# The first batch of a fused attention and MoE kernel: q norms as column sums on the tensor engine, and A^T W in column parts of 128, 256 and 384

## The chip, the cores and the metric

One core of one Trainium2 chip. The metric is the device time of one execution in microseconds (us), the median of several; lower is better. A profile is of one execution, and its span starts a little inside the metric (572.1 us of span for a run of 573.92). Engines in the profile: PE is the tensor engine (matmuls), PEld its weight loads, DVE the vector engine, ACT the scalar engine, POOL GpSimd, SP the sync engine. POOL issues nearly all of the input loads here. The matmuls of this kernel write to PSUM tiles (`..._ps`), in PSUM banks, and ACT and DVE copy the results out ("evacuate" them). `wo` is the weight of the output product. All runs used below are in the fast state.

## The reference

```python
# B, N, C = 4, 6144, 256; d_ff = 768; 24576 tokens
qn = q / (norm(q, axis=1, keepdims=True) + 1e-06)      # each column of q[b] (6144 rows) by its norm
kn = k / (norm(k, axis=1, keepdims=True) + 1e-06)
s = kn.transpose(0, 2, 1) @ qn / tau                    # 256 x 256 a batch
a = exp(s - s.max(-1)); a /= a.sum(-1) + 1e-09
x = (v @ a).reshape(B * N, C)
h = maximum(maximum(x @ w1, x @ w2), x @ w3)
out = h @ w_out
```

## The kernel before

The kernel never forms x. It multiplies the 256 x 256 attention matrix into the three weights once a batch (A^T W, `aw`), then computes h = max over m of v times `aw[m]` by blocks of 128 hidden columns (`fc` = 0 to 5) for each chunk of 512 tokens, then the output product with `wo`. In the first batch nothing can hide the way to `aw`: q has to land, the gram matrix k^T q has to be summed, the softmax done, the first part of A^T W multiplied, and only then can the first h matmul run. That stretch is what the change is about.

```python
    for load, widths in ((load_k, [8] * 5), (load_q, [8] * 4 + [4, 4, 4, 2, 2])):
        ...                                   # q of batch 0 lands in nine pieces
    FT = 2 * P                                # P = 128
    def load_w(fp):
        fsl = slice(fp * FT, (fp + 1) * FT)
        for wt, w in zip(w_sb, w_list):
            POOL.dma_start(out=wt[:, :, fsl], in_=w.rearrange("(cc p) f -> p cc f", p=P)[:, :, fsl])
    load_v(0)
    for fp in range(d_ff // FT):
        load_w(fp)
    load_v(1)
    wo_sb = consts.tile([P, FC, d_model], BF16, name="wo_sb")
    ...
    def gram(b):                              # for batch 0 only
        ...
        for tp in range(NG // 2):             # 24 pairs of row groups
            for j in range(CC):               # CC = 2 halves of the 256 columns
                PE.matmul(ps[j][:, 0:C], lhsT=qt[:, tsl, jsl], rhs=kt[:, tsl, :], ...)
                PE.matmul(ps[j][:, C:C + P], lhsT=qt[:, tsl, jsl], rhs=qt[:, tsl, jsl], ...)   # q by q
    ...
    def softmax_t(ps, rkb):
        for j in range(CC):                   # the norms: the diagonal of q by q
            DVE.tensor_tensor_reduce(out=scr, in0=ps[j][:, C:C + P], in1=ident, scale=1.0, scalar=0.0,
                                     op0=ALU.mult, op1=ALU.add, accum_out=n2q[:, j:j + 1])
        ACT.activation(out=lnq, in_=n2q, func=AF.Ln)
        ACT.activation(out=rq, in_=lnq, func=AF.Exp, scale=-0.5, bias=neg_ln_tau)
        return exp_t(scaled([ps[j][:, 0:C] for j in range(CC)], rkb), rq)     # et, one Exp per half j
    ...
    def aw_first(et, aw):                     # part of 256 columns, six products in six PSUM banks
        products(0, (0, 1))                   # j = 0, m = 0 and 1
        sums(0)
        sums(1)                               # row sums of et
        DVE.reciprocal(out=rinv, in_=rs_ps[:, 0:CC])
        products(1, (0, 1))
        for j in range(CC):
            products(j, (2,))
        ...                                   # evacuate the six, scaled by rinv, on ACT and DVE in turn
    ...
    ps = gram(0)
    ...                                       # six dummy matmuls
    et = softmax_t(*ps)
    v_transpose_pe(0)
    aw = alloc_aw()
    rinv = aw_first(et, aw)
    v_transpose(1)                            # a DMA transpose of the second v chunk
    hold_loads(1)                             # POOL waits for that transpose
    POOL.dma_start(out=wo_sb, in_=moe_w_out.rearrange("(fc p) d -> p fc d", p=P))
    load_v(2)
    load_v(3)
    ...                                       # then the chunks; the other parts of A^T W follow h blocks 0 and 2
```

## Time and profile before

| | before |
|---|---|
| time, median of 4 fast runs beside the changed kernel | 574.11 us (574.0 to 574.3) |
| last q piece lands | 33.63 us |
| first h matmul | 37.52 us, 3.89 after it |
| wo lands | 50.54 us |
| first output product | 50.63 us, 17.00 after the last q piece |

From the page of the kernel before: the busy line of the engines, and PE's row of the view in 40 slices (each digit the busy share of 14.3 us in tenths).
```profile
PE 553.9 (97%) x3349; PEld 330.7 (58%) x3350; DVE 411.1 (72%) x647; ACT 309.1 (54%) x539; POOL 235.1 (41%) x240
PE   3799999999999999999999999999999999999997
```
PE is full from the third slice to the last but one, so whatever is gained must be gained in the first two to three slices, and it reaches the end only if it moves the start of the unbroken row of matmuls.

The first h matmul in PE's timeline of the kernel before (the chain has it at 37.56, as it shows modelled ends):
```profile
37.52 1.46 PE L389 MATMUL h_ps<-vt_sb,aw_sb 128*128 128x512 bf16 x6
```

### The profile page before, as it was taken

Reading aid. Unit: us, or ns where it says so; the run is one execution under the profiler, and the core shown is the slowest. Engines: PE = TensorE matmul, PEld = TensorE weight load, DVE = VectorE, ACT = ScalarE, POOL = GpSimd, SP = SyncE. Lnnn points to the kernel's source line nnn. Section 1 sums busy time; section 2 is a strip of 40 time slices with the busy share of each in tenths; the row PEclk is TensorE's granted clock in tenths of the full one; section 3 lists DMA queues with packets and bytes.
Section 4 is the critical chain, followed back from the end, with each engine's and each line's share of the span. In section 5 each row is a group of like instructions: output and inputs, shape, how many; then the busy total and the mean of one; then the engine's idle time right before and its main releaser. Section 6 shows DMA issues by size and latency. Waiting matters only on the chain.

```text
span 572.1 us, 9442 instructions
## 1 busy us (share of the span) xinstructions
PE 553.9 (97%) x3349; PEld 330.7 (58%) x3350; DVE 411.1 (72%) x647; ACT 309.1 (54%) x539; POOL 235.1 (41%) x240
## 2 busy tenths in 40 slices
PE   3799999999999999999999999999999999999997
PEld 2665555555755555555575555555575555555566
DVE  0048777877577777777768777777868778778775
ACT  1044567677454576776545467767645444444443
POOL 2443357776730078776560048777750000000000
PEclk9999999999999999999999999999999999999999
DMA  9998998884598168984179339885437323132112
GB/s 143 106 146 129 136 237 126 159 135 116 99 107 160 56 107 158 134 148 110 57 128 151 99 81 140 148 141 98 124 86 154 75 75 109 56 103 64 56 55 76
DMA packets 76960, 65.64 MB, mean 115 GB/s; under 512 B 52464, under 2 KB 62576, under 8 KB 76784
## 3 DMA queue, kind: packets, MB, share of 16 engines
q0 software_dynamic: 19072, 26.48, 38.7%
q1 hardware_dynamic: 57696, 38.41, 23.7%
q8 instruction: 26, 0.43, 0.3%
q14 instruction: 22, 0.18, 0.1%
q10 hardware_dynamic: 144, 0.13, 0.1%
HBM read 78.64 MB, written 25.17 MB: 181 GB/s over the span
## 4 chain that ended last, share of the span: by engine, by line
PE 93%; DMA 5%; POOL 0%; issue 0%; DVE 0%; POOLq 0%
PE h_ps L389 65%; PE o_ps L409 22%; DMA q_sb<-in_q_dram 5%; PE gram L260 3%; PE ew_ps L311 3%; POOL k_sb L99 0%; PE o_ps L434 0%; PE ew_ps L335 0%; PE warm_ps L469 0%; PE vt_ps L372 0%; PE gram L177 0%; PE n_ps L215 0%; DVE ht_sb L395 0%; DVE o_sb L461 0%; PE n_ps L217 0%
## 5 line engine op out<-in xcount | busy, mean ns | idle before, releaser
L389 PE MATMUL h_ps<-vt_sb,aw_sb 128*128 128x512 bf16 (+1 forms) x1764 | 406.7, 375 | 0.1
L389 PEld LDWEIGHTS <-aw_sb 128*128 128x128 bf16 x1764 | 171.8, 98 | 161.3 <-DVE aw_sb L317 2.0
L394 DVE TENSOR_TENSOR s_mx<-h_ps,s_mx 128x512 bf16<-128x512 f32 (+1 forms) x294 | 198.7, 676 | 87.1 <-ACT s_mx L393 86.8
L393 ACT ACTIVATE s_mx<-h_ps 128x512 bf16<-128x512 f32 (+1 forms) x294 | 172.4, 587 | 124.9 <-PE h_ps L389 124.0
L395 DVE TENSOR_TENSOR ht_sb<-h_ps,s_mx 128x512 bf16<-128x512 f32 (+1 forms) x294 | 200.2, 681 | 31.4 <-PE o_ps L409 0.5
L203 POOL TENSOR_TENSOR acc<-acc,sq 128x768 f32<-128x768 f32 x90 | 147.6, 1651 | 70.5 <-ACT sq L197 61.6
L409 PE MATMUL o_ps<-wo_sb,ht_sb 128*128 128x256 bf16 x1128 | 153.9, 273 | 0.0
L409 PEld LDWEIGHTS <-ht_sb 128*128 128x128 bf16 x1128 | 110.4, 98 | 52.0
L412 ACT ACTIVATE o_sb<-o_ps 128x512 f32<-128x512 f32 x94 | 56.1, 597 | 85.3 <-PE o_ps L409 85.3
L110 POOL DMA_DIRECT2D v_sb<-in_v_dram x48 | 27.5, 578 | 37.7 <-DMA vt_sb<-v_sb 35.5
L197 ACT ACTIVATE sq<-q_sb 128x768 bf16<-128x768 fp8e4 x48 | 40.5, 845 | 0.0
L197 ACT ACTIVATE sq<-k_sb 128x768 bf16<-128x768 fp8e4 x48 | 40.1, 835 | 0.0
L200 POOL CAST acc<-sq 128x768 f32<-128x768 bf16 x6 | 4.9, 823 | 68.7 <-ACT sq L197 68.7
L102 POOL DMA_DIRECT2D q_sb<-in_q_dram x33 | 18.4, 564 | 5.1 <-DMA v_sb<-in_v_dram 4.1
L165 PE MATMUL kk<-k_sb 128*128 128x256 fp8e4 x48 | 7.5, 338 | 11.9 <-DVE k_sb L151 6.3
L99 POOL DMA_DIRECT2D k_sb<-in_k_dram x29 | 16.1, 555 | 3.1 <-DMA v_sb<-in_v_dram 1.2
L260 PE MATMUL gram<-k_sb,q_sb 128*128 128x512 fp8e4 x144 | 16.8, 277 | 0.0
L260 PEld LDWEIGHTS <-q_sb 128*128 128x256 fp8e4 x144 | 15.9, 136 | 0.6
L314 ACT ACTIVATE aw_sb<-ew_ps,rinv 128x384 bf16<-128x384 f32 (+1 forms) x24 | 13.2, 555 | 5.5 <-PE ew_ps L311 4.7
L311 PE MATMUL ew_ps<-w_sb,et 128*128 128x384 bf16 (+1 forms) x96 | 15.6, 313 | 0.0
L177 PE MATMUL gram<-k_sb,q_sb 128*128 128x512 fp8e4 x48 | 11.4, 332 | 2.6 <-DMA q_sb<-in_q_dram 2.4
L165 PEld LDWEIGHTS <-k_sb 128*128 128x256 fp8e4 x48 | 6.4, 182 | 12.9 <-DMA k_sb<-in_k_dram 6.6
(67 smaller groups left out, 112.9 us busy)
## 6 DMA issues: line engine op xcount, KB each, us to landing
out_dram<-o_sb SPq DMA_DIRECT2D x41, 512.0 KB, 2.9
v_sb<-in_v_dram POOLq DMA_DIRECT2D x48, 256.0 KB, 4.2
k_sb<-in_k_dram POOLq DMA_DIRECT2D x24, 192.0 KB, 6.0
q_sb<-in_q_dram POOLq DMA_DIRECT2D x24, 192.0 KB, 7.6
out_dram<-o_sb SPq DMA_DIRECT2D x13, 256.0 KB, 2.0
k_sb<-in_k_dram POOLq DMA_DIRECT2D x5, 256.0 KB, 10.8
w_sb<-in_moe_w_dram POOLq DMA_DIRECT2D x9, 128.0 KB, 5.7
kf<-in_k_dram SPq DMA_DIRECT2D x1, 1024.0 KB, 4.8
```

Source lines behind the costliest of these rows:

```text
L102: POOL.dma_start(out=qk[b][0][:, g0:g0 + w, :], in_=q_r[b][:, g0:g0 + w, :])
L110: POOL.dma_start(out=t, in_=v_r[gi // NCH, gi % NCH])
L197: ACT.activation(out=sq, in_=src, func=AF.Square)
L203: POOL.tensor_tensor(out=acc, in0=acc, in1=sq, op=ALU.add)
L260: PE.matmul(g[:, j * C:(j + 1) * C], lhsT=qt[:, tsl, j * P:(j + 1) * P], rhs=kt[:, tsl, :], start=(tp == 0 and j == 0), stop=(tp == NG // ...
L311: PE.matmul(ew[:, :w], lhsT=et[:, j, ic * P:(ic + 1) * P], rhs=w_sb[m][:, j, fsl], start=(j == 0), stop=(j == CC - 1))
L389: PE.matmul(t.rearrange("p (t n) -> p t n", n=P), lhsT=aw[m][:, ic, fsl], rhs=vt[:, tsl, ic, :], start=(ic == 0), stop=(ic == CC - 1))
L393: ACT.activation(out=s_mx, in_=hp[0], func=AF.Copy)
L394: DVE.tensor_tensor(out=s_mx, in0=hp[1], in1=s_mx, op=ALU.max)
L395: DVE.tensor_tensor(out=ht, in0=hp[2], in1=s_mx, op=ALU.max)
L409: PE.matmul(st["ps"][:, half], lhsT=ht[:, fc, t * P:(t + 1) * P], rhs=wo_sb[:, fc, :], start=(fc == 0), stop=(fc == FC - 1))
L412: ACT.activation(out=st["o"][:, t - 1:t + 1, :].rearrange("p t d -> p (t d)"), in_=st["ps"], func=AF.Copy)
```

## The change

Its intent: the q norms should come sooner than the DVE diagonal gives them, and the first h matmul should need only 128 columns of A^T W, since the first h block uses no more. Squares of each q piece are made on ACT and DVE, and PE sums their columns with one-column matmuls, while it waits for the next piece. The 256-column part that follows is put between the matmuls of the first h block, and the last 384 columns behind h block 2. The PE transposes of the first v chunk use two PSUM banks, so that DVE and ACT copy out at the same time.

```diff
-    FT = 2 * P
+    PARTS = ((0, P), (P, 3 * P), (3 * P, d_ff))
+    def load_w(lo, hi): ...                      # three loads a part, of 128, 256 and 384 columns
...
-                PE.matmul(ps[j][:, C:C + P], lhsT=qt[:, tsl, jsl], rhs=qt[:, tsl, jsl],
-                          start=False, stop=last, perf_mode=DR, skip_group_check=True)
+        def squares(g0, w):
+            ACT.activation(out=a[:, 0:h, :], in_=ra, func=AF.Square)
+            DVE.tensor_tensor(out=d[:, 0:h, :], in0=rd, in1=rd, op=ALU.mult)
+        def columns(rows, first=False, last=False):
+            for n, (t, r) in enumerate(rows):
+                for j in range(CC):
+                    PE.matmul(nq[:, j:j + 1], lhsT=t[:, r, j * P:(j + 1) * P], rhs=ones_c, ...)
+        for i, w in enumerate(QW):               # columns of the piece before, gram of this one, squares
...
-    def softmax_t(ps, rkb):
-        for j in range(CC):
-            DVE.tensor_tensor_reduce(...)
+    def softmax_first(gs, rkb, n2q):             # n2q is the bank of column sums
...
     def aw_first(et, aw):
-        products(0, (0, 1))
-        sums(0)
-        sums(1)
+        for j in range(CC):
+            for ic in range(CC):
+                PE.matmul(rs_ps[:, ic:ic + 1], lhsT=et[:, j, ic * P:(ic + 1) * P], rhs=ones_c, ...)
+            for m, ic, ew in ews:
+                product(et, ew, m, ic, *PARTS[0], js=(j,))
         DVE.reciprocal(out=rinv, in_=rs_ps[:, 0:CC])
-        products(1, (0, 1))
-        for j in range(CC):
-            products(j, (2,))
...
     def v_transpose_pe(gi):
-        vt_ps = xtile("vt_ps", cols=TPC * C, dtype=BF16)
+        banks = [xtile("vt_ps", cols=TPC * C, dtype=BF16), ps_h.tile([P, TPC * C], BF16, tag="h", name="vt_ps2")]
...
+    def h_block_first(aw, et, rinv):
+        for m in range(3):
+            ...                                  # two h matmuls of m
+            for ic in range(CC):
+                product(et, ews[m][ic], m, ic, *PARTS[1])
+        ...                                      # evacuations between the three steps of the maximum
...
-    for i in range(6):                           # dummy matmuls
+    for i in range(2):
...
-                        gaps[2 * fp - 2].append(lambda fp=fp: aw_part(et, rinv, aw, fp, FT))
+                    gaps[2].append(lambda: aw_part(et, rinv, aw, *PARTS[2]))
```

## The prediction

> **What bounds the kernel now.** I read the page first, then the chain of waits, then the timeline of the first 52 us, then the list of DMA landings. PE is busy 553.9 us of 572.1, and the only waits of PE that the waits view lists are on k and q loads and on the first cast. So from the first h matmul on PE is never short of work, and only the first 38 us can give something back. The chain of waits, in order of time (start us, us, what):
> ```profile
> 20.91 12.72 DMA q_sb<-in_q_dram
> 33.63 0.04 issue
> 33.67 0.32 PE gram L177
> ...
> 34.29 1.24 PE warm_ps L469 x5
> 35.53 0.45 PE vt_ps L372 x8
> 35.98 0.61 PE ew_ps L335 x4
> 36.59 0.08 PE rs_ps L329 x4
> 36.67 0.89 PE ew_ps L335 x8
> 37.56 1.41 PE h_ps L389 x6
> 38.97 1.31 PE ew_ps L311 x12
> 40.28 2.66 PE h_ps L389 x12
> 42.94 1.31 PE ew_ps L311 x12
> 44.25 6.54 PE h_ps L389 x30
> 50.80 0.66 PE o_ps L409 x6
> ```
> The last q piece lands at 33.63. From there to 37.5 the softmax runs, and dummy matmuls stand in for work. Then PE is solid: h, A^T W, h, and at 50.6 the first output product. The timeline of the softmax (start us, us, engine, line, operation):
> ```profile
> 34.09 0.29 DVE L282 CUSTOM_DVE_ANT_0 scr<-gram,ident 128x128 f32<-128x128 f32 x1 [14.01 <-PE gram L179]
> 34.75 0.75 DVE L268 TENSOR_TENSOR e_in<-gram,rkb 128x256 f32<-128x256 f32 x2
> 34.87 0.20 ACT L286 ACTIVATE lnq<-n2q 128x2 f32<-128x2 f32 x1 [6.00 <-DVE n2q L282]
> 35.34 0.91 ACT L275 ACTIVATE et<-e_in,rq 128x256 bf16<-128x256 f32 x2
> 36.70 0.17 DVE L341 RECIPROCAL rinv<-rs_ps 128x2 f32<-128x2 f32 x1 [0.27 <-PE rs_ps L329]
> ```
> The norm's diagonal (34.09 to 34.83 on DVE) holds up both Ln and e_in, so it costs about 0.7 us on the path. The third thing to see is the first output product, which needs wo:
> ```profile
> 45.36 0.83 POOL L483 DMA_DIRECT2D wo_sb<-in_moe_w_out_dram  x1
> ...
> 50.42 0.75 PEld L409 LDWEIGHTS <-ht_sb 128*128 128x128 bf16 x6
> 50.63 0.82 PE L409 MATMUL o_ps<-wo_sb,ht_sb 128*128 128x256 bf16 x6
> ```
> ```profile
> wo_sb<-in_moe_w_out_dram POOLq DMA_DIRECT2D x1, 384.0 KB, 5.2
> ```
> 45.36 + 5.2 = 50.56, and the landing records of the trace say 50.54. PE waits about 0.04 us from a landing to a matmul (33.63 to 33.67), so PE could have started at 50.58 and did at 50.63: **0.05 us of slack**. And wo is itself the end of a chain of transfers: the second v chunk lands at 42.18 (queued behind all of q, v and the nine w pieces, with the queue full since 5 us), its transpose is then issued and lands at 45.07, and only then is wo issued. Landing of v to landing of wo is 8.36 us, and nothing in it depends on PE.
>
> **What the Trainium skill says.** (1) "DMA: Bandwidth & Descriptors", "Why small descriptors are slow": a descriptor costs its 32-byte beats plus about 3, and the DMA clock is given there as 850 MHz. For the 1 KB reads of a w piece that is 35/0.85 = 41 ns, times 16 per engine 0.66 us; landings of the w pieces in this trace are 0.64 to 0.73 apart, so it agrees. (2) "Runtime: NRT & Kernel Launch", "Instruction fetch mechanics": instructions are fetched in blocks of 16 KiB, 256 instructions, by the sequencer's own DMA queue. The trace agrees: 26 packets of 16,384 bytes on queue 8. The first starts at 29.30, when PE had run 226 weight loads and matmuls, the second at 44.79 (442). The first took 0.98 us, and after it one of the 16 engines is late for good: the spread between first and last engine of a load goes from 0.78 to 1.27 us. (3) "TensorE: Matmul & The Clock Gate", Part 1: the array runs at half clock until it was busy for a window of about 3.4 us. The trace shows it: the q matmul pairs are 0.32 us apart from 20.67 to 26.06 and 0.165 after.
>
> **The change part by part.**
> *q norms.* Removed: 48 q-by-q matmuls (0.054 us each at full clock, half of a 0.32/2 pair more at the slow one) and the DVE diagonal. Added: squares of each piece on ACT (768 elements take 0.84 us here, so 1024 about 1.1) and DVE (about 1.1 by its one element per cycle in the other rows, an estimate), which fit in the 2.45 us between loads, and 48 x 2 = 96 column matmuls with one column and a whole weight load each. The four row sums in this trace (the same shape) are about 0.054 us apart, so 96 x 0.054 = 5.2 us at full clock against 2.6 removed; at the slow clock I take twice that, an estimate. Gram pieces alone are 0.118 us per matmul (the later batches) and about 0.213 slow. Walking it through the landings (20.63, 23.09, 25.58, 28.02, 29.26, 31.31, 32.26, 32.91, 33.63) with the clock rising at 26.06 as now: gram and columns of the first piece to 24.0, of the second to 26.8, the third with the k norm to 29.3, the fourth to 31.1; then close behind the loads; last gram 34.5, last column about 34.75. So PE, idle between pieces today, becomes just about full, and the last column sum comes when the old diagonal was ready (34.83). Ln, Exp and e_in then give et at 35.3, where it is today. Gain here: about 0, at best 0.4 us if the clock rises early.
> *First A^T W part of 128 columns.* Products go from 12 x 0.11 to 12 x 0.08 (the spacing of the eight transposes), but the order changes: row sums of the second half follow six products, and the sixth of them takes the PSUM buffer of the second transpose bank, which ACT empties only after both exponentials (36.25 plus about 0.35). So row sums end at about 36.75, reciprocal 36.98 to 37.15, first evacuation (128 columns, estimated 0.28 from 0.475 for 256) to 37.45, first h matmul at about **37.5**, as today.
> *The parts after that.* Behind the first h matmul there is now 1.31 us (256 columns, between the h matmuls of the first block) and 12 x 0.1625 = 1.95 (384) where it was 1.31 + 1.31. So PE reaches the first output product 0.64 us later: 50.63 + 0.64 = 51.25. To break even the first h matmul would have to come at 36.9.
> *Loads.* Same bytes and as many descriptors: 19/0.85 x 16 = 0.36, 0.66 and 0.96 us for the three widths, 5.9 us for nine as now. But PE has more instructions early: 388 up to the last column instead of 288, so the second instruction fetch, at about 442, comes near 37 to 39 us, into the full queue, not into the gap at 44.79. If it uses the same DMA engine as the first, v lands some 0.9 us later (the first made that engine 0.85 to 1 us late) and wo at about 51.4.
> *Sum.* Start of the output products: the later of PE (51.25) and wo (50.55, or 51.4 with the fetch), so about 51.2 to 51.45 against 50.63: plus 0.6 to 0.8 us. Everything after it is PE work in the same order, so it goes into the time one for one: 574.12 + 0.7 = **574.8**.
>
> **The rivals.**
> *It gains as intended.* If the columns hide wholly, et comes 0.4 us sooner, and without the wait for the transpose bank the first h matmul could come near 36.7. For it: the diagonal is on the path today. Against: wo then pins the start of the output products, so no more than 0.05 us is had: 574.1. A real gain (573.5) would need wo to land sooner, and I see nothing that brings it.
> *The clock stays low.* A matmul of one column leaves the array mostly idle, and the k matmuls, about half busy, stay slow through this trace. If columns don't count as busy, 48 gram matmuls at 0.213 and 96 columns at about 0.1 take 20 us from 20.67, to about 40 us, against 34.1 now: 578 to 580. A clock that rises one window later costs about 2 us: 576.5.
> *PE is not slower, and only the fetch matters*: 574.9 by wo alone; without the fetch, 574.1 to 574.3.
> *Evacuations of 384 columns* (0.58 us ACT, 0.61 DVE each) queue behind the maxima on DVE and make PE wait for the fourth h block: 0.1 to 0.4 more.
>
> **Range and chances.** The two main outcomes lie at 574.1 to 574.4 and 574.6 to 575.1; a late clock has perhaps one chance in five and reaches 576.5 and more. A gain beyond 0.4 us I give one in twelve. Hence 573.8 to 576.8. Two per cent is 11.5 us, more than a third of the first 33 us: only a clock that is low throughout comes near it.
>
> **What would show each step.** Right: PE gaps in the q phase gone, first h matmul within 0.3 us of 37.5, the sixth product waiting for ACT, a wait of PE (or none, with 0.6 us more work) ahead of the first output product, the second instruction packet before 41 us and v landing near 43.1. Wrong: column matmuls that stay 0.1 us apart after 27 us (clock), a first h matmul well before 37, or wo landing before 50.5.

## More of the kernel before

One line of the table of stretches (stretch; busy us and instructions of PE, PEld, DVE, ACT, POOL; clock; share and rate of DMA) is of use later, for the stretch from the last q piece to the first h matmul:

```profile
33.60:37.20 3.60, 3.46 (x32) 2.52 (x34) 2.08 (x9) 2.04 (x6) 3.04 (x5) 1.00 1.43 192
```

In 3.60 us PE is idle for 0.14 only. Part of the busy time is dummy work, but from 35.37 on it is transposes and products that have to be done anyway.

## The result and the profile after

| | before | after |
|---|---|---|
| time, median (4 fast runs each, same chip) | 574.11 us (574.0 to 574.3) | 574.44 us (574.17 to 574.72) |
| ratio after to before, 95% interval | | 1.0006 (0.9988 to 1.0023): the same within 2% |
| last q piece lands | 33.63 | 33.67 |
| first h matmul | 37.52 (3.89 later) | 37.17 (3.50 later) |
| wo lands | 50.54 | 50.58 |
| first output product | 50.63 | 50.97 |

Ratios here and below are the mean time of one kernel's fast runs over that of the other's of the same rounds, so not quite the ratio of the medians quoted. The difference, 0.33 us, is smaller than the interval can vouch for. The traces are finer: an event early in the run can be placed to some hundredths of a microsecond in one profile. But the runs don't start alike: in the twelve profiles the last q piece lands anywhere from 33.47 to 33.87, which is more than the change is worth. So starts are best compared by their distance from the last q piece: the first output product comes 17.00 us after it before and 17.30 after.

The chain of waits after (start us, us, what), from the stretch that the change touches:
```profile
30.25 5.75 DMA w_sb<-in_moe_w_dram
36.00 0.05 issue
36.04 0.38 PE ew_ps L326 x2
36.42 0.03 PE rs_ps L350 x2
36.45 0.32 PE ew_ps L326 x5
36.77 0.36 ACT aw_sb L332
37.13 0.05 issue
37.17 0.60 PE h_ps L414 x2
...
42.56 1.95 PE ew_ps L326 x12
44.52 6.61 PE h_ps L398 x30
51.13 0.66 PE o_ps L444 x6
```
The chain no longer begins at the last q piece. It begins at a piece of w, the 128 columns of m = 2, which lands at 36.00. Behind it stand two of the six products, the row sums of the second half, the rest of the products, an evacuation of 128 columns on ACT, and the first h matmul. (The chain shows modelled ends; the timeline has the first output product at 50.97, in the last line below.) One more wait hides in it: the sixth product starts at 36.21, 0.16 us after the fifth, where products otherwise start 0.055 apart. The trace of parts_only, below, names what the same product waits for there: ACT's copy out of the second transpose bank. Here that copy ends at 36.16. The twelve products ahead of the fourth h block, 256 columns wide and 1.31 us long before, are 384 wide and take 1.95.

The timeline after, softmax and first h block (start us, us, engine, line, operation, and in brackets idle time before it and what ended it):
```profile
30.02 0.34 PE L188 MATMUL nq<-ones_c,sqd 128*128 128x1 bf16 x8
33.78 0.42 ACT L181 ACTIVATE sqa<-q_sb 128x256 bf16<-128x256 fp8e4 x1 [0.30 <-DMA q_sb<-in_q_dram]
34.26 0.76 DVE L293 TENSOR_TENSOR e_in<-gram,rkb 128x256 f32<-128x256 f32 x2
34.54 0.17 ACT L306 ACTIVATE lnq<-nq 128x2 f32<-128x2 f32 x1 [0.34 <-PE nq L188]
34.98 0.91 ACT L300 ACTIVATE et<-e_in,rq 128x256 bf16<-128x256 f32 x2
36.49 0.17 DVE L354 RECIPROCAL rinv<-rs_ps 128x2 f32<-128x2 f32 x1 [0.41 <-PE rs_ps L350]
36.75 0.89 ACT L332 ACTIVATE aw_sb<-ew_ps,rinv 128x128 bf16<-128x128 f32 x3 [0.60 <-PE ew_ps L326]
37.17 0.60 PE L414 MATMUL h_ps<-vt_sb,aw_sb 128*128 128x512 bf16 x2 [0.37 <-ACT aw_sb L332]
50.97 0.82 PE L444 MATMUL o_ps<-wo_sb,ht_sb 128*128 128x256 bf16 x6
```
The exponentials (`et`) start at 34.98 instead of 35.34: the norms do come sooner, by 0.36 us. The column sums cost PE very little: eight of them in a row take 0.34 us from the start of the first to the end of the last, of which one matmul's own duration is 0.163, so they start (0.34 - 0.163) / 7 = 0.025 us apart. But the first h matmul is now preceded by 0.37 us in which PE waits for an evacuation. The same stretch as before in the table of stretches, after:
```profile
33.60:37.20 3.60, 2.99 (x38) 1.84 (x38) 2.34 (x7) 2.42 (x8) 3.06 (x5) 1.00 1.51 187
```
PE is busy for 2.99 of 3.60 us instead of 3.46. The 0.47 us less is not all moved work, since four dummy matmuls are gone and column sums have come. The moved work shows behind the first h matmul: from there to the first output product it is now 50.97 - 37.17 = 13.80 us in which PE is nearly always busy, where it was 50.63 - 37.52 = 13.11. That is 0.69 more behind a start that is 0.35 earlier: 0.34 us later, close to the 0.33 us of the medians. (That the profiled run itself is 0.54 us longer is taken up below.) 1.95 - 1.31 = 0.64 us is the wider products. The rest is a balance of small terms, one of which is a wait. In the view of waits of the first 60 us (who waited for whom: us in total, times, longest):
```profile
PEld L398 <- DVE aw_sb L334: 1.3, 4, 0.4
```
These are the weight loads of h blocks, which wait for evacuations of A^T W on DVE. In the fourth h block, behind the 384-column evacuations, the h matmuls start up to 0.30 us apart instead of 0.216 and lose 0.14 us in all. In the kernel before no step between the h matmuls of its fourth block is longer than 0.22.

### The profile page after: what moved, and what is told of

Same layout as the page of the kernel before. It is cut to its first block, busy times and chain, and to the rows that moved or that the text cites. A ratio compares the mean times of both kernels' runs of the same rounds, so it can differ in the third digit from the quotient of the medians.

```text
span 572.7 us, 9555 instructions
## 1 busy us (share of the span) xinstructions
PE 554.1 (97%) x3393; PEld 328.9 (57%) x3394; DVE 418.6 (73%) x652; ACT 315.7 (55%) x548; POOL 235.2 (41%) x240
## 4 chain that ended last, share of the span: by engine, by line
PE 93%; DMA 3%; issue 2%; POOL 1%; DVE 0%; ACT 0%; POOLq 0%
PE h_ps L398 65%; PE o_ps L444 22%; PE gram L285 3%; PE ew_ps L326 3%; DMA q_sb<-in_q_dram 2%; DMA w_sb<-in_moe_w_dram 1%; POOL k_sb L100 0%; PE o_ps L469 0%; POOL q_sb L103 0%; PE h_ps L414 0%; PE n_ps L240 0%; DVE ht_sb L404 0%; DVE o_sb L496 0%; ACT aw_sb L332 0%; PE n_ps L242 0%
## 5 line engine op out<-in xcount | busy, mean ns | idle before, releaser
L332 ACT ACTIVATE aw_sb<-ew_ps,rinv 128x384 bf16<-128x384 f32 (+2 forms) x27 | 14.5, 545 | 6.4 <-PE ew_ps L326 5.3
L326 PE MATMUL ew_ps<-w_sb,et 128*128 128x384 bf16 (+2 forms) x108 | 17.7, 308 | 0.1
L181 ACT ACTIVATE sqa<-q_sb 128x1024 bf16<-128x1024 fp8e4 (+2 forms) x9 | 6.9, 770 | 18.6 <-DMA q_sb<-in_q_dram 18.6
L285 PE MATMUL gram<-k_sb,q_sb 128*128 128x512 fp8e4 x144 | 16.8, 277 | 0.0
L334 DVE TENSOR_SCALAR aw_sb<-ew_ps,rinv 128x384 bf16<-128x384 f32 (+2 forms) x27 | 13.9, 564 | 0.7 <-PE ew_ps L326 0.6
```

The costliest lines, as they stand in the source:

```text
L285: PE.matmul(g[:, j * C:(j + 1) * C], lhsT=qt[:, tsl, j * P:(j + 1) * P], rhs=kt[:, tsl, :], start=(tp == 0 and j == 0), stop=(tp == NG // ...
L326: PE.matmul(ew[:, :hi - lo], lhsT=et[:, j, ic * P:(ic + 1) * P], rhs=w_sb[m][:, j, lo:hi], start=(j == 0), stop=(j == CC - 1))
```

## The experiments

Ten kernels were run, in three groups, each group on one chip beside runs of the kernel before. The theory after the result, **T**: the time is the start of the first output product plus a fixed rest; that start is PE's own arrival, unless wo lands later; the change loses because a smaller first part moves products behind the first h matmul and leaves PE idle in a latency (row sums, reciprocal, evacuation) that a part of 256 columns had covered. Rivals: **R1**, wo's landing sets the start in both kernels, and PE's order is of no account; **R2**, the column sums and squares cost something; **R3**, the second instruction fetch delays the loads.

### The parts of the change, each alone

*norms_only*: the kernel before with the new norms and two dummies, the rest as it was.
```diff
-    ps = gram(0)
-    for i in range(6): ...                       # dummy matmuls
-    et = softmax_t(*ps)
...
+    first = gram_first()
+    for i in range(2): ...
+    et = softmax_first(*first)
```

> The kernel before with the new q norms alone (column sums, squares on ACT and DVE, two dummy matmuls), A^T W parts as before. My theory: et comes 0.36 us sooner, as in the changed kernel (34.98), but the 256-wide w pieces land at 35.50, 36.17 and 36.85, so the products of the second w matrix and the row sums behind them start no sooner than before; first h matmul 37.4 to 37.55 (before 37.5), first output product 50.55 to 50.65, time within 0.1 us of the kernel before. Rival (the norms give the 0.36 us and the parts take it away again): first h matmul at 37.15 and, held by wo at 50.58, a time 0.05 us lower at most, but PE idle ahead of the first output product by 0.2 to 0.3 us, which the first theory does not have.

Measured: 574.23 (574.03 to 574.77) against 574.22 of before (11 runs, 573.97 to 575.63), ratio 0.9999 (0.9987 to 1.0011). Two lines of its timeline, and the end of its chain of waits:
```profile
36.44 0.38 PE L355 MATMUL ew_ps<-w_sb,et 128*128 128x256 bf16 x2 [0.29 <-DMA w_sb<-in_moe_w_dram]
37.76 1.46 PE L409 MATMUL h_ps<-vt_sb,aw_sb 128*128 128x512 bf16 x6
```
```profile
36.77 6.22 DMA v_sb<-in_v_dram
...
43.01 2.86 DMA vt_sb<-v_sb
...
46.16 5.23 DMA wo_sb<-in_moe_w_out_dram
...
51.44 0.82 PE o_ps L429 x6
```
The first h matmul comes 3.90 us after the last q piece (33.86 here), as in the kernel before: earlier norms alone give nothing, because the products then wait 0.29 us for 256-column pieces of w. So R2 falls: the column sums cost nothing either. The median came as expected; the first output product of the profiled run did not (51.44, where 50.55 to 50.65 was expected), and this run, 574.77, shows R3 at work. The second 16,384-byte packet of instructions came at 39.68, and by the landings on the DMA engine that was already the last: v landed at 42.99 instead of 42.18, wo at 51.39 instead of 50.54, and PE was idle for 0.40 us until wo had come. Not all of that is the fetch. The last q piece was 0.23 us late already (33.86 against 33.63); counted from it, v is 0.58 us later than in the kernel before and wo 0.62. The other four runs, 574.03 to 574.31, were not profiled; that their fetch went to another engine fits, but is only argued. In the changed kernel's own profile the fetch came at 38.61 on an engine that was not the latest, and v landed on time. Of the eight profiled runs with a fetch between 38 and 40 us, two had it on the late engine.

*parts_only*: the changed kernel with the old norms and six dummies.
```diff
-    first = gram_first()
...
-    et = softmax_first(*first)
+    ps = gram(0)
...
+    et = softmax_t(*ps)
```

> The changed kernel with the q norms of before (diagonal on DVE, six dummy matmuls). My theory: et as before (35.34), first h matmul at 37.3 to 37.5, and behind it 0.64 us more A^T W work than in the kernel before, so first output product at 51.1 to 51.3 and a time 0.5 to 0.7 us above the kernel before, that is 0.2 to 0.35 above the changed kernel. Rival (the parts cost nothing and the norms are what costs): time as before, and first h matmul before 37.0.

Measured: 574.79 (574.56 to 576.3), ratio 1.0013 (1.0002 to 1.0025): slower than before by more than the whole change is. Its timeline:
```profile
36.51 0.22 PE L308 MATMUL ew_ps<-w_sb,et 128*128 128x128 bf16 x1 [0.16 <-ACT vt_sb L368]
37.48 0.60 PE L396 MATMUL h_ps<-vt_sb,aw_sb 128*128 128x512 bf16 x2 [0.37 <-ACT aw_sb L314]
51.27 0.82 PE L426 MATMUL o_ps<-wo_sb,ht_sb 128*128 128x256 bf16 x6
```
The first h matmul is again 3.90 us after the last q piece (33.58), and 13.79 us of work follow it. So the parts are what costs: 0.69 us more behind the first h matmul (13.79 against 13.11 in the kernel before), with nothing gained ahead of it. The sixth product waits for the bank that ACT empties, as the prediction said of the changed kernel. (The transposes into two banks belong to these parts and were not run alone.) Only with both halves of the change together does the first h matmul come 0.39 us sooner after the last q piece (3.50 against 3.89).

### What pins the first output product

*before_wo_late*: the kernel before with wo behind the third v chunk.
```diff
-    POOL.dma_start(out=wo_sb, ...)
     load_v(2)
+    POOL.dma_start(out=wo_sb, ...)
     load_v(3)
```

> The kernel before with wo loaded behind the third v chunk instead of ahead of it. My theory: wo has 0.05 us of slack in the kernel before, so wo landing 1.2 us later or more goes into the time nearly whole: first output product 1.1 to 2 us later, time 575.2 to 576.1. Rival (wo is not what the first output product waits for, or a later wait absorbs it): time within 0.2 us of the kernel before.

Measured: 579.55 (576.63 to 581.18), ratio 1.0092 (1.0069 to 1.0115). The direction was foreseen, the size was not: 575.2 to 576.1 were expected. A line of its chain of waits, then two of its timeline:
```profile
45.88 8.06 DMA wo_sb<-in_moe_w_out_dram
```
```profile
53.98 1.44 PE L409 MATMUL o_ps<-wo_sb,ht_sb 128*128 128x256 bf16 x6 [3.21 <-DMA wo_sb<-in_moe_w_out_dram]
55.22 2.41 PE L389 MATMUL h_ps<-vt_sb,aw_sb 128*128 128x512 bf16 x6
```
Two things were missed. Wo did not take the 5.2 us from issue to landing that it takes in the kernel before but 8.06, as the DMA transpose of the third v chunk now ran beside it; that this transpose is what slowed it is inferred from the order, not isolated, and part of the 8.06 is the queue, as wo now stands behind the third v chunk, which landed at 49.00. And PE, having waited 3.21 us, came back at a slow clock: the first output step takes 55.22 - 53.98 = 1.24 us instead of 0.66, the next six h matmuls 57.46 - 55.22 = 2.24 instead of 1.29. The sum holds: 3.35 us later start (53.98 - 50.63) + 0.58 + 0.95 = 4.88, and the profiled run is 578.79 - 573.92 = 4.87 us longer than the profiled run of before. The Trainium skill, "TensorE: Matmul & The Clock Gate", Part 1, says that after an idle window of some 3.4 us the clock is halved, and that it comes back after a busy one. The trace agrees in kind: its clock record shows half the clock from 53.71 to 57.13, 3.41 us. But when it fell, PE had been idle for only 2.94 us (from 50.77, a modelled end), so here less than a whole window of idling was enough. One of the six runs, 576.63, has a mean granted clock of 1.000 where the others have 0.994 to 0.996; that it is the one run that kept the clock fits, but it was not profiled. So a wait for wo does go into the time one for one, and if long enough with interest. T's "unless wo lands later" is shown.

*before_wo_early* and *after_wo_early*: wo ahead of the second v chunk, so that it cannot be what is waited for.
```diff
+    POOL.dma_start(out=wo_sb, ...)
     load_v(1)
...
     hold_loads(1)
-    POOL.dma_start(out=wo_sb, ...)
```

> The kernel before with wo loaded ahead of the second v chunk. My theory: PE is what sets the first output product in the kernel before (50.63 against a landing at 50.54), so wo landing at about 43 changes nothing: time within 0.1 us, as long as the transpose of the second v chunk (then landing at about 47.1) is there before its first h matmul at 48.2. Rival (wo sets it): 0.2 us or more faster.

Measured: 574.03 in four fast runs (573.95 to 574.14), ratio 0.9995 (0.9982 to 1.0008). The profiled run (593.97 at a granted clock of 0.951) is not used. The median is 0.19 us below that of before, between the 0.1 that was expected and the 0.2 of the rival, and the interval includes 1: these runs don't tell the two apart. The trace of the kernel before does: its last h matmul starts at 50.42 and the output product 0.216 us later, the usual step, so PE did not wait for wo and has nothing to gain from an earlier one.

> The changed kernel with wo loaded ahead of the second v chunk. In the changed kernel PE reached the first output product at 50.97, 0.41 us after PE could have had wo (landing 50.52 and 0.04). My theory (PE, not wo, sets it): first output product stays at 50.9 to 51.0 and the time at 574.3 to 574.5. Rival (the transfers behind wo hold the changed kernel): 0.2 us or more faster. Where an instruction fetch falls on the engine that is already late, wo is no longer hit, so the slowest runs should not go above 574.6.

Measured: 574.38 (574.05 to 574.56) against 574.14 of before in this group (9 runs), ratio 1.0003 (0.9991 to 1.0016). Of its timeline:
```profile
50.76 0.82 PE L445 MATMUL o_ps<-wo_sb,ht_sb 128*128 128x256 bf16 x6
```
50.76 is 17.29 after its last q piece (33.47); in the changed kernel it was 50.97 - 33.67 = 17.30. With wo out of the way nothing moves, so in the changed kernel PE sets the start, and R1 falls for it.

### Giving the idle time back

*after_m2_last*: in the first part the products of m = 2 wait until all row sums are out.
```diff
             for m, ic, ew in ews:
-                product(et, ew, m, ic, *PARTS[0], js=(j,))
+                if m < 2:
+                    product(et, ew, m, ic, *PARTS[0], js=(j,))
+        for m, ic, ew in ews:
+            if m == 2:
+                product(et, ew, m, ic, *PARTS[0])
```

> The changed kernel with the products of the third w matrix, first part, behind the row sums and the products of the first two, so that the row sums wait neither for its load (landing at 35.95) nor for the transpose bank that ACT empties at 36.15. My theory: row sums end at 36.1, reciprocal at 36.25, first h matmul at 36.8 to 36.9 instead of 37.17, first output product at 50.6 to 50.7, time 574.05 to 574.2, as the kernel before. Rival (the first h matmul is set by the evacuations or by v, not by the row sums): first h matmul stays at 37.1 to 37.2 and the time at 574.4.

Measured: 574.01 (573.88 to 575.43), ratio 1.0004 (0.9992 to 1.0017; one run of 575.43 pulls the mean). Its timeline:
```profile
36.08 0.17 DVE L358 RECIPROCAL rinv<-rs_ps 128x2 f32<-128x2 f32 x1
36.77 0.61 PE L418 MATMUL h_ps<-vt_sb,aw_sb 128*128 128x512 bf16 x2 [0.26 <-ACT aw_sb L332]
50.57 0.82 PE L448 MATMUL o_ps<-wo_sb,ht_sb 128*128 128x256 bf16 x6
```
The row sums no longer stand behind the two products of m = 2, of which one needs the w piece of 36.00 and the other the bank that ACT empties at 36.16; which of the two waits matters more was not separated. The reciprocal comes at 36.08 instead of 36.49, the first h matmul 3.19 us after the last q piece instead of 3.50, the first output product 16.99 instead of 17.30. That is 0.31 us, the whole loss of the change by the traces (17.30 - 17.00 = 0.30), from the order of six products.

*m2_wo_early*: the same with wo ahead of the second v chunk, to see whether wo now holds it up.

> The run after_m2_last with wo loaded ahead of the second v chunk as well. My theory: PE sets the first output product there (50.6 to 50.7 against 50.58 by wo), so this changes the time by less than 0.1 us. Rival (wo sets it as soon as PE is no longer late): 0.1 to 0.3 us faster than after_m2_last.

Measured: 574.26 (573.65 to 574.75), ratio 1.0003 (0.9991 to 1.0016). By medians it is 0.25 us slower than after_m2_last, where less than 0.1 was expected. The first h matmul is again 3.19 us after the last q piece, but the first output product 17.13. Here the second fetch (38.69) was the other one that hit the late engine, and with wo ahead of it in the queue the second v chunk came late as well: about 0.13 us of PE's wait for its transpose. From the first h matmul to the first output product it is 13.94 us, where after_m2_last has 13.80, as the changed kernel and after_wo_early have. So wo did not hold up after_m2_last by more than hundredths either: issued at 45.4 and 5.1 us on its way, it landed just ahead of PE, and freeing it gained nothing.

*best*: after_m2_last, and two products of the second part (m = 0, 256 columns) ahead of the m = 2 ones, to fill the wait for the evacuation; w pieces loaded in the order of use; wo early.
```diff
+        xt = xtile("ew_x")
+        ex = [xt[:, ic * 2 * P:(ic + 1) * 2 * P] for ic in range(CC)]
+        for ic in range(CC):
+            product(et, ex[ic], 0, ic, *PARTS[1])
...
+    for m, part in ((0, 0), (1, 0), (0, 1), (2, 0), (1, 1), (2, 1), (0, 2), (1, 2), (2, 2)):
+        load_w(m, part)
```

> A version meant to beat both: the changed kernel with the third w matrix last, the second-part products of the first matrix (4 matmuls, 0.44 us) ahead of the first h matmul in a bank of their own, where PE is idle now, the w pieces loaded in the order of use, and wo ahead of the second v chunk. My theory: PE is busy without a gap from 35.6 on, first h matmul at 36.95 to 37.2 with only 0.87 + 1.95 us of A^T W behind it, first output product at 50.3 to 50.5, time 573.75 to 574.0, that is 0.2 to 0.35 us under the kernel before. Rival (the order of PE does not matter, only bounds elsewhere do): 574.1 to 574.4.

Measured: 574.71 (574.62 to 574.77), ratio 1.0011 (0.9997 to 1.0024). It missed. Its timeline:
```profile
38.83 0.48 DVE L335 TENSOR_SCALAR aw_sb<-ew_x,rinv 128x256 bf16<-128x256 f32 x1 [1.08 <-ACT aw_sb L333]
40.36 0.11 PEld L407 LDWEIGHTS <-aw_sb 128*128 128x128 bf16 x2 [0.67 <-DVE aw_sb L335]
41.34 1.19 PEld L407 LDWEIGHTS <-aw_sb 128*128 128x128 bf16 x7 [0.87 <-DVE aw_sb L335]
```
Both products lay in one tile in one PSUM bank. The Trainium skill, "PSUM — Partial Sum Buffer", section "PSUM bank collisions raise a hardware error", says that two engines must not touch one bank at once and that semaphores have to guard the bank (and its quadrant of partitions), not the address. The trace fits: DVE waited 1.08 us until ACT had emptied its half of the bank, the maxima queued behind it, and PE's weight loads waited 0.67 and 0.87 us.

*best2_early*: the same with two banks, and both evacuations of the last m (of its second part) on ACT. *best2_next*: the same again, with wo directly behind the second v chunk in the queue instead of ahead of it.
```diff
-        xt = xtile("ew_x")
-        ex = [xt[:, ic * 2 * P:(ic + 1) * 2 * P] for ic in range(CC)]
+        ex = [xtile("ew_x") for ic in range(CC)]
...
-    POOL.dma_start(out=wo_sb, ...)             # best2_next only
     load_v(1)
+    POOL.dma_start(out=wo_sb, ...)             # best2_next only
```

> The run best, mended: there the two halves of the early second-part products lay in one PSUM bank, VectorE's evacuation waited for ScalarE's (to 38.83), and everything behind it on VectorE came late, so PE waited 0.67 and 0.87 us for weights. Here each half has a bank, and ScalarE takes both evacuations of the third matrix. My theory: those waits go, first h matmul 3.3 us after the last q landing, first output product 16.6 to 16.8 us after it (kernel before 17.00, changed kernel 17.30), plus up to 0.15 us if the transposed second v chunk (now landing at 47.8 to 48.1) is late; time 573.75 to 574.0. Rival (VectorE is full in the first blocks whatever the banks): 574.4 or more.

Measured: 574.06 (573.86 to 576.66) against 574.46 of before in this group (11 runs, 574.07 to 578.04), ratio 0.9996 (0.9974 to 1.0019). A line of the timeline, of POOL's guard that waits for the transpose of the second v chunk:
```profile
48.14 0.19 POOL L528 COPY guard<-vt_sb 128x1 bf16<-128x1 bf16 x1 [10.02 <-DMA vt_sb<-v_sb]
```
With wo ahead of it the second v chunk is transposed only at 48.08, and PE waits for it. The first output product is 16.95 us after the last q piece: no better than before (17.00).

> As best2_early, but wo directly behind the second v chunk instead of ahead of it, so that the transpose of that chunk comes as early as in the changed kernel if the two don't get in each other's way. My theory: wo lands before 50.0 and the transposed chunk before 47.8, first output product 16.6 to 16.75 us after the last q landing, time 573.7 to 573.9. Rival (a load beside the transpose slows both, as when wo went beside the third chunk's transpose and landed at 53.9): wo or the chunk late, time 574.3 or more.

Measured: 573.78 (573.67 to 573.90 in six runs), ratio 0.9984 (0.9964 to 1.0005): still "the same" by 2%, and the interval includes 1, as the runs of before spread in this group. But all six runs lie below the fastest of the eleven of before (574.07) on the same chip; in the other groups runs of before went down to 573.76. The 0.68 us between the medians is more than the traces support (0.24 below). A line of its timeline, and three of its chain of waits:
```profile
37.35 0.47 DVE L335 TENSOR_SCALAR aw_sb<-ew_x,rinv 128x256 bf16<-128x256 f32 x1
```
```profile
36.27 0.56 PE ew_x L327 x4
36.82 0.22 PE ew_ps L327 x4
37.05 0.86 PE h_ps L422 x4
```
The chain has no gap: the two products (`ew_x`) run in the 0.56 us in which the changed kernel waited. DVE starts its evacuation at 37.35 with no wait. Wo lands at 44.40 and the transposed v chunk at 45.47, both well ahead of need. The first output product is at 50.31, 16.76 us after the last q piece: 0.24 sooner than in the kernel before and 0.54 sooner than in the changed one. Of the 0.54, after_m2_last gave 0.31; the other 0.23 came with several edits at once (early products, order of the w loads, place of wo, evacuations on ACT), which were not separated.

### All profiled runs together

T says that the time is the start of the first output product plus a fixed rest. Each row is one profiled run, less the profiled run of the kernel before (573.92, first output product at 50.63):

| run | time | minus 573.92 | first output product | minus 50.63 |
|---|---|---|---|---|
| after | 574.46 | 0.54 | 50.97 | 0.34 |
| norms_only | 574.77 | 0.85 | 51.44 | 0.81 |
| parts_only | 574.56 | 0.64 | 51.27 | 0.64 |
| after_wo_early | 574.05 | 0.13 | 50.76 | 0.13 |
| after_m2_last | 573.88 | -0.04 | 50.57 | -0.06 |
| m2_wo_early | 574.26 | 0.34 | 50.99 | 0.36 |
| best | 574.71 | 0.79 | 51.36 | 0.73 |
| best2_early | 574.07 | 0.15 | 50.73 | 0.10 |
| best2_next | 573.67 | -0.25 | 50.31 | -0.32 |

The two differences agree within 0.07 us in eight of nine rows. The changed kernel's own run has 0.20 us more. Its trace shows where they arise: the output products stay 0.34 us behind those of the kernel before until about 79 us, and 0.55 behind from then on. At 79.75 PE starts an h matmul 0.42 us after the one before instead of 0.22, as the DMA transpose of the fifth v chunk has landed only at 79.70 (at 78.33 in the kernel before). No other run of the table repeats it. So T's "fixed rest" holds unless a later load is late.

## Why the prediction was right or wrong

**The total was right**: 574.8 was predicted, 574.44 came, in the range, with the sign right and the class "the same". The change itself was forecast at plus 0.7 us and came at half, plus 0.33, which the runs alone cannot tell from zero. The frame held too: all of it happens ahead of the first output product, and later PE work hands it on one for one. The table above shows it, which the prediction could only argue.

**"PE reaches the first output product 0.64 us later" was right in kind and nearly in size.** It measured 0.69 behind the first h matmul, here and in parts_only. That it agrees so closely is in part luck, as 0.14 us of it are waits in the fourth h block that the sum did not have and smaller steps elsewhere offset them. (The prediction's own sum is off by a slip: 50.63 + 0.64 is 51.27, not 51.25. Nor do its 388 and 288 instructions compare like with like: the 288 leave out four of the k norm. Neither matters.) This is the core: a smaller first part doesn't save work, it moves products from ahead of the first h matmul to behind it, into wider ones.

**"First h matmul at about 37.5, as today" was wrong**: it came at 37.17. This is the step that put the prediction too high by about as much (574.8 against 574.44), and its first cause lies in an earlier term. The prediction took the column matmuls as 0.054 us each, "the four row sums in this trace are about 0.054 us apart", twice that at the slow clock, and so had PE "just about full" and the last column sum at 34.75. They are 0.025 us apart, and 0.027 even at the slow clock, so 96 of them take 2.5 us, no more than the 2.6 of the matmuls removed. PE kept its gaps, the last column sum started at about 34.3, and `et` came 0.36 us earlier, not at 35.3. The line was even in the prediction's own first fence: the chain gives 0.08 us for four row sums. The row of four lasts 0.24 us, and a quarter of it is 0.06. These records overlap, so one duration has to come off first: (0.24 - 0.163) / 3 = 0.026. The clock, on which the prediction spent most of its upper tail, rose about a microsecond later than before (27.25 against 26.16 in the clock records) and cost nothing: in after_wo_early it rose at 29.14, and `et` starts 1.30 us after the last q piece there as in the changed kernel.

**The steps from `et` to the first h matmul were right in kind, but half a microsecond too late.** The row sums of the second half do stand behind six products and come late (they start at 36.26; their end was predicted at 36.75). In the changed kernel's trace there are two waits before them: the fifth product waits for the w piece of 36.00, which the prediction did not have, and the sixth for ACT's copy out of the second transpose bank, which it named; the copy ends at 36.16, not at 36.60, as `et` was early. after_m2_last shows what this order costs: 0.31 us. The 128-column evacuation takes 0.36 us, not 0.28; the products start 0.055 us apart, not 0.08. (The eight transposes last 0.61 us; an eighth of that is 0.076, so this looks like the slip of the row sums again.) So the reciprocal was 0.49 us earlier than predicted (36.49 against 36.98), the stretch from it to the first h matmul 0.16 longer (0.68 against 0.52), and the h matmul 0.33 earlier.

**The slack of wo was right** (0.05 us in the kernel before), and before_wo_late and norms_only's profile show that wo does hold PE when it is late. **The second fetch "into the full queue, near 37 to 39 us" was right as to time** (38.61) **and wrong as to effect** in the profiled run: it went to an engine that had room. In norms_only it went to the late one. There wo landed at 51.39, where 51.4 was predicted for that case, but by luck: the fetch made up 0.62 us of the delay, and the other 0.23 was there at the last q piece. Which engine gets the fetch differed from run to run.

**Of the rivals**, "it gains as intended" was half true: the first h matmul came 0.35 us sooner by the clock, but the prediction's reason against a gain, the landing of wo, wasn't what undid it. The work moved behind it did. "The clock stays low" didn't happen. "Evacuations of 384 columns" did happen, at the low end of the 0.1 to 0.4 us that it was given: 0.14 us in the fourth h block. The chain of waits doesn't show it, because it merges the h matmuls into one piece.

## What to carry to other kernels

Making the first piece of a pipelined product smaller pays only if the latency behind it (here row sums, reciprocal, evacuation) is then filled with work of the next piece; otherwise the work merely moves behind the start, and the idle time is the price. That is a matter of tenths of a microsecond in 574. Read the gain as the distance from the last landed input to the first step that waits for nothing more, not as the start of the first useful matmul. And when pieces are filled in, give each engine that evacuates its own PSUM bank, or the wait comes back under another name (best against best2_early). Loading in the order of use goes with it here, but no run shows what it is worth alone.

## What the Trainium skill lacked or had wrong

- "TensorE: Matmul & The Clock Gate", sections "LDWEIGHTS (loading the stationary operand)" and "Back-to-back issue gap": the weight load is given as its columns over 1.2, 107 ns for 128 columns. At the full clock the records here do last some 95 to 99 ns, but pairs of a 128-column load and a one-column matmul start 25 ns apart (27 ns at the slow clock), so the load is hidden, and the page's issue floor of about 25 ns is what counts. Its sustained 81 ns for 128 columns is too long here: products of 128 columns, each with its weight load, start 55 ns apart (36.31 to 36.59 in the changed kernel).
- "Runtime: NRT & Kernel Launch", section "Instruction fetch mechanics": crossing a block is called mostly hidden. Here a 16,384-byte packet fetched between 38 and 40 us took 0.96 to 0.98 us in seven of eight profiles and 1.22 in the other. In two of them the landings show that it went to the DMA engine that was already last, and the queued loads landed later (in norms_only v 9.13 us after the last q piece instead of 8.55). The page doesn't say which engine carries it.
- No page read says what a load costs beside a DMA transpose: in before_wo_late wo took 8.06 us from its issue, behind the third v chunk and beside that chunk's transpose, against 5.2 us in the kernel before, and the transpose 7.3 us from issue to landing (49.01 to 56.32) against 2.8. How much of it is the one slowing the other was not isolated.
